# Attention and ELU-MoE on one core: a new hand-laid order, W1 loaded by other groups of columns, two V casts moved to GpSimd

## The chip, the core and the metric

The kernel runs on one core of a Trainium2 chip. A core has five engines that run side by side: TensorE (matmuls into PSUM, "PE" in the profile), VectorE ("DVE"), ScalarE ("ACT"), GpSimd ("POOL") and SyncE ("SP", which here only issues DMAs). DMA queues move data between HBM and SBUF. The metric is the device time of one execution in microseconds; before the change it is 303.02 us, the median of three runs (303.0 to 303.15).

## What is computed

The reference, cut to what matters:

```python
# q, k, v: (8 batches, 8 heads, 576 tokens, 64), fp32
q_s = exp(q - max_d q);  q_s /= sum_d q_s          # softmax over the head dimension
k_s = exp(k - max_s k);  k_s /= sum_s k_s          # softmax over the tokens
kv  = einsum('bhsd,bhse->bhde', k_s, v)            # 64 x 64 a head
att = einsum('bhsd,bhde->bhse', q_s, kv)
x   = att.transpose(0, 2, 1, 3).reshape(4608, 512)
h   = x @ w_in                                     # 512 -> 2048
g   = where(h > 0, h, exp(min(h, 0)) - 1)          # ELU
out = g @ w_out                                    # 2048 -> 512
```

## The kernel before

**Two streams of work.** The attention goes by units: a unit is one batch and half of the heads, so there are 16, numbered n, two a batch. The product with w_in and w_out goes by blocks of 512 tokens: 9 blocks, numbered j. A ring XT of three blocks holds attention's output, transposed, for the products.

**A unit** (`stage1` and after it): loads of Q, K and V (576 KB each); exp of Q and of K on ScalarE (L355, L359); a cast of V to bf16 into VB (L368 on ScalarE, L371 on another engine); on VectorE the row sums of Q, their reciprocals and the scaled Q as fp16 (L375, L379, L383: QS). QS is transposed: in units 0 to 3 by TensorE (`tp`, L406), with a copy out of PSUM to qsT; from unit 4 on by a DMA issued by SP (`turn`, L422) and widened to fp32 by ScalarE (`widen`, L434). K times V is a block of 36 small matmuls (`kv_mm`, L458); VectorE scales the result to MBLK (`m`: L467, two of L471). Then `ao_mm` (L489) multiplies MBLK by qsT, and `xt` copies the result to XT (L511 on ScalarE, L514 on VectorE).

**A block** has eight groups g of 256 columns of w_in. `hg_mm` (L545) is one group: eight matmuls of 512 columns into one of four pairs of PSUM banks. `hg` empties it: exp on ScalarE (L561), two VectorE operations (L578, L580), or, in every other group of blocks 0 and 1, a second ScalarE operation (L572) and one of VectorE (L574); the result is GT. Then `out_mm` (L590) multiplies GT by w_out, 64 matmuls a block, into four output tiles; `out_store` copies a tile out of PSUM (L607, OSBX in block 0, OSB later), and SP stores it (L617). In block 0 the output tiles are made in quarters, each of which needs one of four loads of w_out (W2, 1 MB each).

**The start.** SP loads Q, K and V of units 0 and 1. GpSimd's queue loads w_in (W1) behind them, in pieces by groups: 0-2 (in two halves of the rows, so that the first half's product can begin once unit 0 is done, since unit 0 gives one half of XT's rows and unit 1 the other), 3-4 and 5-7. Each piece is two DMAs. `hg_mm` with `half` set is half a group, four matmuls. In the first microseconds TensorE gets spin matmuls on the identity (L655) where the planner sees it idle; their number follows from the planner's times.

**The order.** Every operation has an index, given by the place where `program` adds it. The table ORDER has one line of indices for each engine, and each engine runs its operations in just that order. `Sched.order` walks through the five lines with estimated durations and latencies; from the estimated starts come the interleaving in which code is emitted, and the number of spin matmuls (`fill`). Semaphore waits follow from the tiles that operations read and write. An engine works in order: what stands behind a waiting instruction waits too. The same holds for the DMA issues in the lines of SP and GpSimd. GpSimd's line in the old table, from index 57 on, reads: Q of unit 2, W2 part 0, W2 part 1, Q of 3, V of 2, K of 2, W2 part 2, K of 3, the V cast of unit 2, W2 part 3, V of 3, V of 4, Q of 4, Q of 5, the V cast of unit 3, K of 4, V of 5, K of 5. V of units 2, 4 and 5 share one buffer, so V of unit 5 can only be loaded once V of unit 4 has been cast; K of unit 4 needs unit 2's K times V to be done, K of unit 5 that of unit 3.

Where V is cast is chosen in `first`: `vconv="gp" if n < CASTS else "act"`, with CASTS = 4; units 0 and 1 have their own setting (CAST0, CAST1). W1 is loaded by

```python
for g0, g1, half in ((0, 3, 0), (0, 3, 1), (3, 5, None), (5, 8, None)):
    self.load_w1(g0, g1, half, -30, [gate, self.ident] if half == 0 else ())
```

where `gate` is the load of K of unit 0.

Of the kernel before, what the change touches and what calls it, by code (L numbers as in the profile page):

```python
# [19 lines left out]
CASTS = 4  # L20
# [4 lines left out]
        "30 28 32 45 43 47 50 68 54 67 70 71 69 72 82 86 93 103 115 128 90 129 130 138 137 107 131 "  # L25
        "139 136 109 150 149 126 134 151 132 157 158 156 140 152 153 146 173 175 172 159 174 233 239 "
        "238 237 243 192 244 245 250 251 249 201 256 257 203 255 263 262 212 261 268 267 269 321 309 "
        "313 317 333 220 325 338 329 350 334 280 399 282 342 346 291 391 351 395 299 412 400 404 408 "
        "362 417 364 425 413 430 421 438 373 479 426 381 434 487 500 439 450 483 492 452 488 496 505 "
        "461 501 513 469 509 526 514 518 522 564 538 527 568 540 572 577 549 573 581 585 590 556 594 "  # L30
        "586 598 607 599 603 640 611 636 612 644 622 649 624 645 657 653 632 670 634 662 658 666 675 "
        "683 688 679 671 709 692 714 696 684 705 701 697 718 735 710 731 740 722 727 723 744 748 761 "
        "736 753 766 749 757 774 779 762 770 787 775 783 788 792 793 797 801 805 "),
    "act": (
        "3 22 33 23 31 24 34 29 44 35 48 55 73 76 77 79 83 84 87 94 95 104 97 116 117 119 91 92 108 "
        "98 127 120 133 135 163 166 160 181 154 147 179 205 230 231 169 176 189 180 234 188 240 241 "
        "191 246 273 252 253 202 258 211 204 264 213 265 215 270 284 214 310 314 218 217 318 221 322 "
        "355 279 326 339 330 294 281 335 290 283 343 347 292 297 293 392 296 352 300 396 366 376 401 "
        "361 375 363 405 379 409 443 378 418 454 414 365 372 374 431 422 427 382 435 480 466 449 440 "
        "464 451 484 531 542 493 489 453 460 463 506 497 462 467 502 510 470 515 519 537 523 565 551 "  # L40
        "539 528 552 569 541 548 550 578 574 555 582 616 554 595 587 557 608 626 604 591 600 641 621 "
        "613 637 623 625 631 646 650 654 633 659 663 667 676 689 635 680 672 693 685 706 698 715 702 "
        "719 732 711 741 728 724 745 737 750 754 767 758 763 780 771 776 784 789 794 798 802 806 808 "),
    "dve": (
        "4 5 0 6 7 2 25 26 27 37 38 39 40 41 42 46 36 49 51 52 53 56 74 75 78 80 81 85 88 89 96 105 "
        "106 100 101 102 122 123 124 118 110 111 112 141 142 143 155 148 182 183 184 232 177 178 206 "
        "235 207 236 208 193 242 194 195 196 197 247 198 248 254 259 274 275 260 266 276 271 272 311 "
        "285 312 286 319 320 287 356 222 223 327 224 328 225 226 331 227 332 336 337 357 358 344 345 "
        "348 349 353 354 301 397 398 302 367 402 303 304 368 305 306 403 369 410 411 444 455 445 456 "
        "415 446 416 423 424 383 384 385 386 387 428 429 388 457 436 437 441 442 485 486 532 490 533 "  # L50
        "491 498 499 543 503 504 534 471 472 511 473 512 474 516 475 544 476 517 545 524 525 529 530 "
        "570 571 575 583 584 617 576 618 619 596 597 588 589 558 559 609 610 560 601 602 642 627 643 "
        "561 562 628 563 629 614 615 647 648 655 656 660 668 669 661 681 682 673 674 694 695 686 687 "
        "707 708 699 700 720 721 712 733 713 734 725 726 746 738 739 747 751 759 752 760 764 765 772 "
        "773 777 778 785 786 "),
    "gp": (
        "1 14 15 16 17 18 19 20 21 59 57 58 63 61 60 62 64 99 66 65 125 113 144 121 114 186 145 "),
    "sp": (
        "8 9 10 11 12 13 165 162 167 187 164 185 200 210 171 161 209 168 170 190 199 216 278 315 277 "
        "324 219 288 316 341 228 229 289 295 360 298 359 323 307 340 377 308 394 371 406 370 393 419 "  # L60
        "447 407 390 389 380 433 420 448 432 459 482 458 494 465 481 495 478 477 535 468 520 546 566 "
        "567 536 508 553 507 579 547 521 592 580 620 630 639 605 593 652 638 651 606 690 678 664 677 "
        "665 703 717 691 704 729 742 716 730 743 755 769 781 756 790 791 768 782 795 799 796 804 803 "
        "800 807 "),
# [3 lines left out]
class Op:  # L68
    __slots__ = ("eng", "dur", "emit", "deps", "key", "idx", "start", "end",
                 "dma", "sem", "val", "clock", "nbytes", "follow", "side", "late", "packet", "margin",  # L70
                 "gate", "span", "behind")

    def __init__(self, eng, dur, emit, key, dma=None, nbytes=0):
        self.eng, self.dur, self.emit, self.key = eng, dur, emit, key
        self.deps = {}
        self.dma, self.nbytes = dma, nbytes
        self.start = self.end = None
        self.behind = None
        self.follow, self.side, self.packet, self.margin = None, 0, 4608, 0


class Sched:
# [3 lines left out]
    LAT = {"pe": 200, "act": 138, "dve": 116, "gp": 155}  # L86
    LAND = 350
    RESTART = 110
# [40 lines left out]
    def order(self):  # L129
# [4 lines left out]
        while any(line.values()):  # L134
            before = len(seq)
            for e in self.ENG:
                while line[e]:
# [6 lines left out]
                    wake = self.RESTART if e == "pe" and t > free[e] + 30 else 0  # L144
                    o.start, o.end = t, t + o.dur + wake
# [11 lines left out]
    def hop(self, d, o):  # L157
        if d.dma:
            return 30
        if d.eng == o.eng and (d.eng == "pe" or o.deps[d] == "war"):  # L160
            return 0
        return self.LAT[d.eng]

# [79 lines left out]
class Gen:  # L243
# [85 lines left out]
    def load_w1(self, g0, g1, half, key, after=()):  # L329
        w = self.w_in.rearrange("(h kc d) f -> h d kc f", h=2, d=D)  # L330
        sl = slice(g0 * 256, g1 * 256)
        ks = slice(0, 4) if half is None else slice(2 * half, 2 * half + 2)
        xs = (0, 1) if half is None else (half,)
        for h in range(2):
            self.S.add("gp", ISSUE["gp"], lambda e, h=h: e.dma_start(
                self.W1[h:128:2, ks, sl], w[h, :, ks, sl]), key,
                W=[f"W1_{g}{x}{h}" for x in xs for g in range(g0, g1)],
                dma=f"w1{g0}{xs[0]}{h}", nbytes=(len(xs) * (g1 - g0) << 17) * (1.25 if g0 == 3 else 1), after=after,
                follow=self.gpq)
            self.gpq = self.S.ops[-1]  # L340
# [86 lines left out]
    def widen(self, n, key):  # L427
# [3 lines left out]
        if n < CASTS:  # L431
# [5 lines left out]
    def side(self, ps, key, *parts):  # L437

        def mm(e):
            for p in parts:  # L440
# [3 lines left out]
                   X=[f"b{2 * ps}", f"b{2 * ps + 1}"], side=1)  # L444

    KV = 382

    def kv_mm(self, n, ps, at=KV):
        i = n % 2
# [11 lines left out]
        return 510 if at == self.KV else 280, [f"kR{i}", f"VB{i}", f"VB{i}x", f"VBone{i}"], mm  # L461
# [160 lines left out]
    def program(self):  # L622
# [10 lines left out]
        for g0, g1, half in ((0, 3, 0), (0, 3, 1), (3, 5, None), (5, 8, None)):  # L633
# [115 lines left out]
        for half in range(2):  # L749
            for g in range(3):  # L750
                self.hg_mm(0, g, turns[g], key, half)
                S.ops[-1].follow = kv1
        for g in range(8):
            self.hg(0, g, turns[g], key, "da"[g % 2], g > 2)
# [86 lines left out]
```

## Time and profile before

| what | value |
|---|---|
| median of 3 runs | 303.02 us |
| profiled execution | 302.01 us |
| its span, first to last instruction | 300.2 us |
| mean granted TensorE clock | 0.997 |
| first matmul of L545 | 15.42 us |
| last matmul ends | about 296.7 us |
| GpSimd (POOL) busy | 20.2 us, 31 instructions |
| bytes by the two main DMA queues | 34.09 MB and 15.47 MB |

The profile is of one execution, slower or faster than the median by what runs differ. Lines of it read: engine, source line, operation, written tile <- read tiles, shapes, count. In the timeline the first column is the start and the second the length, both in us; what stands in brackets is the idle time of the engine before the row and what ended it. The chain of waits is followed back from the last instruction, at each step to what released it; its rows are start, length, what. DMA rows end with the KB of one and the median us from issue to landing. Idle time of an engine that does not bound the kernel costs nothing. Profiled lengths of matmuls overlap; the distance from one start to the next is what one costs.

### The profile page before, as it was taken

To read this page: it belongs to the slowest core of one execution; us is meant where nothing else is said; L and a number is where in the kernel's file an instruction comes from. 1 tells how busy PE (TensorE), PEld (TensorE's weight loads), DVE (VectorE), ACT (ScalarE), POOL (GpSimd) and SP (SyncE) were. 2 spreads that over 40 slices of the span, in tenths; PEclk is the share of its full clock that TensorE was granted. 3 is DMA by queue.
4 is the path that set the end of the run, shared out by engine and by line. 5 is a ranking of instruction groups with operands and counts; after the bars stand their busy time and mean duration, and the time that the engine had idled before them with its cause. 6 is when DMAs were issued, how large, how long until landed. Compare 5 with 4: busy or idle time off the path is not lost.

```text
span 300.2 us, 4428 instructions
## 1 busy us (share of the span) xinstructions
PE 286.4 (95%) x1855; PEld 234.2 (78%) x1855; DVE 189.0 (63%) x244; ACT 182.7 (61%) x213; POOL 20.2 (7%) x31
## 2 busy tenths in 40 slices
PE   0799999999999999999999999999999999999995
PEld 0678887777888888888888878888888888888883
DVE  3858934987896596787687567675344546356500
ACT  5858759988976889668937664555441543233311
POOL 0950343000000000000000000000000000000000
PEclk9999999999999999999999999999999999999998
DMA  7999999795769697368477730324030032111133
GB/s 265 385 400 388 391 340 328 232 215 211 214 154 330 177 244 218 81 213 291 131 174 180 212 114 2 75 57 107 0 86 2 0 72 60 27 36 36 35 88 87
DMA packets 35283, 49.96 MB, mean 166 GB/s; under 512 B 16320, under 2 KB 16320, under 8 KB 35264
## 3 DMA queue, kind: packets, MB, share of 16 engines
q1 hardware_dynamic: 29680, 34.09, 41.1%
q0 software_dynamic: 5504, 15.47, 15.9%
q8 instruction: 14, 0.23, 0.3%
q10 hardware_dynamic: 80, 0.13, 0.1%
q14 instruction: 5, 0.04, 0.0%
HBM read 36.70 MB, written 9.44 MB: 154 GB/s over the span
## 4 chain that ended last, share of the span: by engine, by line
PE 88%; ACT 6%; DMA 3%; DVE 2%; issue 0%; SPq 0%
PE PS L590 41%; PE PS L545 41%; PE PS L489 3%; PE PS L458 2%; DMA out_dram<-OSB 2%; ACT QR L355 1%; DMA QR<-in_q_dram 1%; ACT ESB L561 1%; PE PS L406 1%; ACT VB L368 1%; ACT KR L359 1%; PE PS L655 1%; ACT OSB L607 1%; DVE QS L383 0%; DVE ZQ L375 0%; ACT XT L511 0%
## 5 line engine op out<-in xcount | busy, mean ns | idle before, releaser
L590 PE MATMUL PS<-W,GT 128*128 128x512 f32 x576 | 141.7, 392 | 0.0
L545 PE MATMUL PS<-XT,W 128*128 128x512 f32 x576 | 140.4, 392 | 0.7 <-ACT OSBX L607 0.6
L545 PEld LDWEIGHTS PS<-XT,W 128*128 128x128 f32 x576 | 106.8, 188 | 24.4 <-ACT OSBX L607 1.0
L590 PEld LDWEIGHTS PS<-W,GT 128*128 128x128 f32 x576 | 106.6, 188 | 22.2 <-ACT OSB L607 0.6
L561 ACT ACTIVATE ESB<-PS 128x1024 f32<-128x1024 f32 x72 | 73.6, 1027 | 64.5 <-PE PS L545 64.4
L578 DVE TENSOR_SCALAR ESB<-ESB 128x1024 f32<-128x1024 f32 x64 | 44.1, 690 | 70.6 <-ACT ESB L561 70.4
L580 DVE TENSOR_TENSOR GT<-ESB,PS 128x1024 fp32r<-128x1024 f32 x64 | 77.6, 1218 | 1.7
L607 ACT ACTIVATE OSB<-PS 128x512 f32<-128x512 f32 x32 | 18.8, 598 | 23.6 <-PE PS L590 19.0
L511 ACT ACTIVATE XT<-PS 128x512 fp32r<-128x512 f32 (+6 forms) x32 | 19.3, 607 | 15.3 <-PE PS L489 13.9
L375 DVE TENSOR_REDUCE ZQ<-QR 128x18 f32<-128x1152 f32 x16 | 21.5, 1346 | 6.0 <-ACT QR L355 6.0
L383 DVE TENSOR_TENSOR QS<-QR,RZQ 128x1152 f16<-128x1152 f32 x16 | 21.7, 1355 | 0.3
L355 ACT ACTIVATE QR<-QR 128x1152 f32<-128x1152 f32 x16 | 18.4, 1166 | 3.0 <-DMA QR<-in_q_dram 3.0
L359 ACT ACTIVATE KR<-KR 128x1152 bf16<-128x1152 f32 x16 | 18.6, 1163 | 1.2 <-DMA KR<-in_k_dram 1.2
L434 ACT ACTIVATE qsT<-QT 128x1152 fp32r<-128x1152 f16 x12 | 14.0, 1170 | 3.3 <-DMA QT<-QS 2.7
L368 ACT ACTIVATE VB<-VR 128x1152 bf16<-128x1152 f32 (+1 forms) x14 | 15.9, 1132 | 0.0
L489 PE MATMUL PS<-qsT,MBLK 128*128 128x320 f32 (+5 forms) x64 | 14.0, 305 | 0.3 <-DVE MBLK L471 0.2
L489 PEld LDWEIGHTS PS<-qsT,MBLK 128*128 128x128 f32 x64 | 11.6, 189 | 3.4 <-DVE MBLK L471 0.6
L574 DVE SCALAR_TENSOR_TENSOR GT<-PS,ESB 128x1024 fp32r<-128x1024 f32 x8 | 9.8, 1222 | 3.0 <-ACT ESB L572 2.9
L406 PE MATMUL PS<-ID,QS 128*128 128x128 f16 x36 | 3.2, 243 | 8.9 <-DVE QS L383 8.9
L471 DVE TENSOR_TENSOR MBLK<-PS,RZK 64x128 fp32r<-64x128 f32 x32 | 9.2, 287 | 0.9
L406 PEld LDWEIGHTS PS<-ID,QS 128*128 128x128 f16 x36 | 2.4, 109 | 9.3 <-DVE QS L383 8.9
L572 ACT ACTIVATE ESB<-ESB 128x1024 f32<-128x1024 f32 x8 | 8.5, 1060 | 0.2
(28 smaller groups left out, 57.9 us busy)
## 6 DMA issues: line engine op xcount, KB each, us to landing
out_dram<-OSB SPq DMA_DIRECT2D x63, 128.0 KB, 2.4
QR<-in_q_dram SPq DMA_DIRECT2D x12, 576.0 KB, 4.7
KR<-in_k_dram SPq DMA_DIRECT2D x12, 576.0 KB, 5.1
VR<-in_v_dram SPq DMA_DIRECT2D x12, 576.0 KB, 5.2
W<-in_moe_w_out_dram POOLq DMA_DIRECT2D x4, 1024.0 KB, 16.1
QR<-in_q_dram POOLq DMA_DIRECT2D x4, 576.0 KB, 11.2
VR<-in_v_dram POOLq DMA_DIRECT2D x4, 576.0 KB, 7.5
KR<-in_k_dram POOLq DMA_DIRECT2D x4, 576.0 KB, 13.1
```

The source lines that it names most:

```text
L355: S.add("act", t_act(1152, False), lambda e: e.activation(flat(q), flat(q), AF.Exp), key - 3, X=[f"qR{i}"], follow=self.table)
L359: S.add("act", t_act(1152, False), lambda e: e.activation(ek[:, :, :, :].rearrange("p h c d -> p (h c d)"), flat(k), AF.Exp), key - 2, X=[ ...
L375: S.add("dve", t_dve(1152), lambda e: e.tensor_reduce(self.ZQ[i][:, :, :].rearrange("p h c -> p (h c)"), q[:, :, :, :].rearrange("p h c d ...
L383: S.add("dve", t_dve(1152), lambda e: e.tensor_tensor(qso, q[:, :, :, :], rz, ALU.mult), key - 3, R=[f"qR{i}", f"RZQ{i}"], W=[f"QS{self.al ...
L489: last = e.matmul(P[:, y:y + n_], M[:, f, :], T[:, c0:c1, f * 64:f * 64 + 64], start=True, stop=True)
L511: S.add("act", t_act((h1 - h0) * n_, True), lambda e, dst=dst, src=src: e.activation(dst, src, AF.Copy), key, W=W, X=X)
L545: last = e.matmul(P[:, t * 512:(t + 1) * 512], self.W1[:, kc, tt * 128:(tt + 1) * 128], self.XT[:, kc, rc:rc + BLK], start=(kc == 0), stop ...
L561: S.add("act", t_act(1024, True), lambda e: e.activation(esb[:, :], P[:, :], AF.Exp), key, W=[f"E{i}"], X=banks)
L578: S.add("dve", t_dve(1024, 2), lambda e: e.tensor_scalar(esb[:, :], esb[:, :], 1.0, -1.0, ALU.min, ALU.add), key, X=[f"E{i}"])
L580: S.add("dve", t_dve(1024), lambda e: e.tensor_tensor(gt, esb[:, :], P[:, :], ALU.max), key, R=[f"E{i}"], W=gw, X=banks)
L590: last = e.matmul(dst, GT[:, jj, ts * 128:(ts + 1) * 128], self.W2[:, jj, :], start=(jj == 0), stop=(jj == 15))
L607: S.add("act", t_act(512, True), lambda e: e.activation(osb[:, :], src, AF.Copy), key, W=[f"O{i}0", f"O{i}1"], X=[f"b{bk}"])
```

## The change

W1 comes in pieces of groups 0-1 (in two halves), 2-4 and 5-7. So only groups 0 and 1 of block 0 are computed in halves, and group 2 is one whole product of eight matmuls. CASTS is 6: the V casts of units 4 and 5 go to GpSimd. `widen` asked the same constant and now asks for `n < 4`; as it is only called from unit 4 on, widening stays on ScalarE. The planner's estimates change: latencies by engine, with 160 ns more for a wait of TensorE and 35 ns for others, in place of a fixed latency and a restart charge; K times V is put at 615 or 290 ns in place of 510 or 280; a block of such matmuls may count as done 200 ns early; the surcharge on a W1 piece moves from 3-4 (1.25) to 2-4 (1.15). A planner's hint that half products follow unit 1's K times V is gone. The table ORDER is replaced by another, solved for two sets of durations together.

```diff
-CASTS = 4
+CASTS = 6
...
     "gp": (
-        "1 14 15 16 17 18 19 20 21 59 57 58 63 61 60 62 64 99 66 65 125 113 144 121 114 186 145 "),
+        "1 14 15 16 17 18 19 20 21 57 59 58 60 63 61 62 66 98 64 65 112 113 124 120 144 143 180 185 "
+        "188 "),
...
-    LAT = {"pe": 200, "act": 138, "dve": 116, "gp": 155}
+    OVER = {"pe": 163, "act": 105, "dve": 82, "gp": 110}
...
-                    wake = self.RESTART if e == "pe" and t > free[e] + 30 else 0
-                    o.start, o.end = t, t + o.dur + wake
+                    o.start, o.end = t, t + o.dur
...
-        if d.dma:
-            return 30
-        if d.eng == o.eng and (d.eng == "pe" or o.deps[d] == "war"):
+        if d.eng == o.eng and not d.dma and (d.eng == "pe" or o.deps[d] == "war"):
             return 0
-        return self.LAT[d.eng]
+        return (0 if d.dma else self.OVER[d.eng] - d.early) + (160 if o.eng == "pe" else 35)
...
-                dma=f"w1{g0}{xs[0]}{h}", nbytes=(len(xs) * (g1 - g0) << 17) * (1.25 if g0 == 3 else 1), after=after,
+                dma=f"w1{g0}{xs[0]}{h}", nbytes=(len(xs) * (g1 - g0) << 17) * (1.15 if g0 == 2 else 1), after=after,
...
-        if n < CASTS:
+        if n < 4:
             self.S.add("gp", 1500, lambda e: e.tensor_copy(dst, src), key, R=["QT"], W=W)
...
+        self.S.ops[-1].early = 200 * any(p[0] > 600 for p in parts)
...
-        return 510 if at == self.KV else 280, [f"kR{i}", f"VB{i}", f"VB{i}x", f"VBone{i}"], mm
+        return 615 if at == self.KV else 290, [f"kR{i}", f"VB{i}", f"VB{i}x", f"VBone{i}"], mm
...
-        for g0, g1, half in ((0, 3, 0), (0, 3, 1), (3, 5, None), (5, 8, None)):
+        for g0, g1, half in ((0, 2, 0), (0, 2, 1), (2, 5, None), (5, 8, None)):
...
-            for g in range(3):
+            for g in range(2):
                 self.hg_mm(0, g, turns[g], key, half)
-                S.ops[-1].follow = kv1
         for g in range(8):
-            self.hg(0, g, turns[g], key, "da"[g % 2], g > 2)
+            self.hg(0, g, turns[g], key, "da"[g % 2], g > 1)
```

The first parts of the four other lines of ORDER, old against new:

```diff
     "pe": (
-        "30 28 32 45 43 47 50 68 54 67 70 71 69 72 82 86 93 103 115 128 90 129 130 138 137 107 131 "
+        "30 28 32 45 43 47 50 67 54 68 69 70 77 81 85 92 114 102 89 128 136 127 135 129 137 106 130 "
...
     "act": (
-        "3 22 33 23 31 24 34 29 44 35 48 55 73 76 77 79 83 84 87 94 95 104 97 116 117 119 91 92 108 "
+        "3 22 33 23 24 29 31 34 35 44 48 55 71 74 75 78 82 83 86 93 94 96 103 115 90 91 118 97 116 "
...
     "dve": (
-        "4 5 0 6 7 2 25 26 27 37 38 39 40 41 42 46 36 49 51 52 53 56 74 75 78 80 81 85 88 89 96 105 "
+        "4 0 5 2 6 7 25 26 27 37 38 39 40 41 42 36 49 46 51 52 53 56 72 73 76 79 80 84 87 88 95 99 "
...
     "sp": (
-        "8 9 10 11 12 13 165 162 167 187 164 185 200 210 171 161 209 168 170 190 199 216 278 315 277 "
+        "8 9 10 11 12 13 184 186 161 164 163 170 167 189 199 198 208 166 169 160 209 215 276 277 315 "
```

To read them: 24 is the V cast of unit 0, 29 and 31 are the two copies of its transposed Q; 36 is VectorE's half of the V cast of unit 1, 46 its half of the copy of unit 1's transposed Q, 49 and 56 its halves of XT of units 0 and 1; 40 to 42 and 51 to 53 scale K times V of units 0 and 1; 32 and 50 are those K times V, 47 and 54 the products with MBLK. 67 and 68 are the first halves of groups 0 and 1 of block 0 in both tables. Above 81 the new table's index is the old one less one: at the seam of blocks 0 and 1 TensorE's line reads 173 175 172 159 174 in the old table and 172 174 158 171 173 in the new one, that is, the last quarter of the last output tile of block 0 comes ahead of the first half of group 0 of block 1. In the same place ScalarE's new line has the exp of unit 4's Q (178) ahead of the XT copies of unit 3 (153, 146), and GpSimd's new line reads from 57 on: W2 part 0, Q of unit 2, W2 part 1, K of 2, Q of 3, V of 2, W2 parts 2 and 3, the V cast of unit 2, K and V of 3, Q, K and V of 4, the V cast of unit 3, K and Q of 5, the V cast of unit 4, V of 5, the V cast of unit 5.

## The prediction

> **What bounds the kernel now.** I read the page's busy table first:
>
> ```profile
> span 300.2 us, 4428 instructions
> PE 286.4 (95%) x1855; PEld 234.2 (78%) x1855; DVE 189.0 (63%) x244; ACT 182.7 (61%) x213; POOL 20.2 (7%) x31
> ```
>
> TensorE is the bound. In the chain of waits 16 matmuls of 512 columns take 3.63 us in quiet stretches, 0.2267 each; 1152 of them are 261 us. They run from 15.42 to 296.67, 281.3 us, and the 20 us between are attention's own matmuls and short restarts. So a new order can win only where TensorE really waits, and the start-to-start times show few such places: the head before 15.42, 0.73 us at 52.96, 0.28 at 177.2, and some 0.12 each after a block of small matmuls. The head by the timeline:
>
> ```profile
> 12.65 0.61 DVE L471 TENSOR_TENSOR MBLK<-PS,RZK 64x128 fp32r<-64x128 f32 x2
> ...
> 13.29 0.69 DVE L416 CAST qsT<-PS 128x512 fp32r<-128x512 f16 x1
> ...
> 14.02 0.76 DVE L371 CAST VB<-VR 128x576 bf16<-128x576 f32 x1
> ...
> 14.69 0.68 DVE L514 CAST XT<-PS 128x512 fp32r<-128x512 f32 x1
> ...
> 15.42 1.21 PE L545 MATMUL PS<-XT,W 128*128 128x512 f32 x4
> ```
>
> VectorE is a solid chain here; the first product waits for its half of XT. Under the head the DMA queues run at about 395 GB/s, so the landings of W1 matter. The DMA view, cut at single issues, of the two loads of groups 3-4 (issued at 10.50 and 11.12), the pair of groups 5-7, and what else ran from 18 to 20 us:
>
> ```profile
> W<-in_moe_w_in_dram POOLq DMA_DIRECT2D x1, 512.0 KB, 7.3
> ```
> ```profile
> W<-in_moe_w_in_dram POOLq DMA_DIRECT2D x1, 512.0 KB, 9.5
> ```
> ```profile
> W<-in_moe_w_in_dram POOLq DMA_DIRECT2D x2, 768.0 KB, 11.5
> ```
> ```profile
> q8 instruction: 1, 0.02, 3.6%
> ```
>
> The first lands at 17.82, the second at 20.61: 2.79 us for 0.52 MB, where 395 GB/s needs 1.33. Of its sixteen semaphore increments fifteen are there by 19.17; the last comes 1.44 us later, right after a 16 KB instruction packet began at 18.41 on one DMA engine. The later loads keep that lag (5-7 ends at 24.54). Before, nothing paid for it: group 3 starts near 21.6, group 5 near 25.2.
>
> **The change part by part.** Above 81 an index of the new table is the old one less one, since one half product is gone (I name operations, not indices). What the planner's constants change is the order and the number of spin matmuls; no other instruction.
>
> *Head.* ScalarE now casts V of unit 0 before it copies the transposed Q. V landed at 2.27 + 6.84 = 9.1, so the cast (1.16) ends at 10.3 instead of 11.2, and K·V can be done by about 11.5. VectorE, free at 11.81 (10.45 + 1.36), need not idle until 12.45: M of unit 0 ends at 12.65 instead of 13.26. Then VB1 0.76, XT 0.69 (ahead of the qsT copy now), qsT 0.69, M of unit 1 0.81: 15.7 instead of 16.19. ScalarE's half of XT still comes near 14.8, so the first product starts near 14.85, and the second half of the first group at 17.35 to 17.6 instead of 17.87. The spin before K·V shrinks from 18 to an estimated 8 to 10 matmuls of 107 ns, but some now stand before the transposes, hence the spread. **-0.4 us.**
>
> *W1.* Groups 0-1 take 1.05 MB instead of 1.57 first; both halves were early anyway (14.52 and 16.48), worth nothing. But group 2 now needs the whole 2-4 load, whose end is the same 2.62 MB into the stream as that of 3-4: 19.17 without the lag, 20.61 with it. TensorE wants it at 17.47 + 8 x 0.2267 + 0.11 = 19.39. Where would the fetch fall? It came after 131 matmul records, ten of them main ones; with a similar spin it comes at the tenth main matmul again, near 17.9. The Trainium skill (Runtime: NRT & Kernel Launch, section on instruction fetch mechanics) calls the cost of crossing a 16 KB block "mostly hidden". By that rule group 2 has its data at 19.2 and waits for nothing; by the row it waits 1.27 and starts at 20.66, where the same point before was 17.87 + 1.92 = 19.79. I take the row: **+0.87 net of the head.** Groups 5-7, at 24.54, are wanted at 26.1 then: free.
>
> *W2 and loads on POOL's queue.* W2's last quarter is issued before the V cast of unit 2, not behind it (36.41 before), and lands near 38.64 + 2.7 = 41.3 instead of 42.77; K and V of unit 3 move behind and land near 42.8 and 44.3 (40.09 and 44.23 before). V of unit 3 is what its K·V waits for, so nothing moves. K of unit 2 comes 3 us earlier, V 1.5 us later (35.98; its cast ends by 37.9, wanted at 39.6).
>
> *The boundary of block 0 and 1.* The chain of waits there:
>
> ```profile
> 48.51 0.74 ACT XT L511 x2
> 49.24 2.11 ACT QR L355 x2
> 51.35 0.92 ACT ESB L561
> ...
> 52.30 1.06 ACT ESB L572
> 53.36 0.49 ACT OSBX L607
> ...
> 53.90 3.94 PE PS L545 x16
> ```
>
> TensorE waited for ScalarE to empty a bank of the last output tile. That tile is now computed before, not after, the first half of group 0, so its copy has 1.8 us of cover: **-0.85** (0.73 and a 0.12 restart). What is late next is ScalarE itself. It loses V's cast of units 4 and 5 (2 x 1.05 in the chain's pitch), but the exp of unit 4's Q (1.05) now stands ahead of unit 3's XT copies, which group 1's second half needs: about +0.4. And two exps (unit 5's Q and K) stand before the exp of group 2 of block 1, as a cast and an exp did before; followed by its two VectorE steps (0.69 + 1.22) it frees group 4's banks at 60.3 to 61.1, against the start at 60.57 now: 0 to +0.7. Together **+0.6**, bounds 0 and +1.1.
>
> *Casts on GpSimd.* The two rows there are
>
> ```profile
> 34.54 1.92 POOL L371 CAST VB<-VR 128x1152 bf16<-128x1152 f32 x1 [15.70 <-DMA VR<-in_v_dram]
> ...
> 44.28 1.15 POOL L371 CAST VB<-VR 128x1152 bf16<-128x1152 f32 x1 [4.25 <-DMA VR<-in_v_dram]
> ...
> 48.61 0.72 POOL L318 DMA_DIRECT2D VR<-in_v_dram  x1 [2.51 <-ACT VB L368]
> ```
>
> The Trainium skill (SBUF — State Buffer, section on the two separate sides) speaks against this: a GpSimd operation and a VectorE one with two SBUF inputs lock a shared port pair for a whole instruction. The slow row stands beside the Q multiplication at 34.10 (1.36), the fast one alone, so the lock explains 0.77. By the rows two casts cost 2.3 to 3.8 us of GpSimd, hidden while V is in time; by the rule, if each meets a full 1.36, some 5.0. The order is what counts: V of unit 5 is issued behind unit 4's cast, which stands behind the loads of K and Q of unit 5, and K's waits for unit 3's K·V (47). So cast 4 ends at 50 to 51, V of unit 5 is issued then, not at 48.61, lands near 55.5 (54.62 before) and is cast by 57.4, when the K·V of units 4 and 5 is wanted at 58.7. No cost by a 1.3 us margin. Widening stays on ScalarE as it was: zero. SP's queue starts with unit 4's transpose ahead of block 0's stores; their tiles are overwritten only near 70 us.
>
> *The rest.* Counting matmuls between two uses of a bank pair in both tables, the least cover is 3.47 us in both, so I expect no new steady stall; the 0.28 at 177 probably goes. -0.2, bounds -0.4 and +0.8.
>
> **Sum**, against the profiled execution's 302.01 (its span 300.2 and 1.8 around it): +0.87 - 0.85 + 0.6 - 0.2 = +0.4, 302.4. The median of the runs is 303.02, so **303.4**.
>
> **Rivals.** *The fetch misses the load* (301.9): if the instruction packet comes after about 18.6, or very early on a lane with slack, group 2 starts on time: -0.4 - 0.85 + 0.3 - 0.2 = -1.1. For it: the fetches come at irregular distances (94 to 339 PE instructions), and a shorter spin delays the count by up to ten matmuls. Against: both loads of the stream stay in flight from 11 to 19 us, a wide target. *GpSimd's chain sets the pace* (304.4): the load of V of unit 5 lands after 57, because the new K and Q loads and block 0's stores go ahead of it, or both casts meet VectorE's two-input steps; then K·V of units 4 and 5 stands at the head of TensorE's order and holds everything, about +1.0 on the forecast. It decides from 1.3 us of lateness on. For it: POOL works in order and three waits are now strung on it. Against: the load took 6.0 us to land before, and 6.5 may pass now. *A stall elsewhere* (from 304): the table is new in some 200 places of TensorE's order and I have followed the first 62 us only.
>
> **Chances.** Forecast 0.40, fetch misses 0.28, GpSimd's chain 0.25, elsewhere 0.07. About 0.2%, 0.6 us, is what a measurement of this kernel can tell from no change. The first rival gives 0.24 of faster, the forecast's lower edge (its own range is 302.7 to 304.1) 0.06: 0.30 faster; the two slow cases and the forecast's upper edge give 0.36 slower; 0.34 within. The range 301.7 to 304.7 takes in both main rivals.
>
> **What would show it.** First main product near 14.85, second half near 17.5; a wait of TensorE of about 1.3 us at the fifth group of eight or so, near 20.6, ended by a W load (none: first rival); no wait near 53 for OSBX; ScalarE's exp of unit 4's Q between OSBX and XT; a TensorE wait for GpSimd's VB near 59 means the second rival. I am wrong in kind if TensorE loses time after 62 us, or if its clock is granted late because the spin is shorter.

## The result and the profile after

The kernel after the change takes **302.0 us** in the median (301.67 to 302.45); the kernel before, on the same chip, 303.01. The ratio is 0.997, with a 95% interval of 0.9957 to 0.9983. So the change made the kernel faster by about 1 us, where 0.4 us slower, 303.4, was forecast; 302.0 lies inside the stated range of 301.7 to 304.7, but on the other side of no change. A later measurement of the two unchanged kernels gave 302.03 against 302.85, ratio 0.9978 [0.9965, 0.999].

One thing has to be seen before any line of the profile is compared. The profiled execution of the kernel after took 302.05 us, as its median. That of the kernel before took 302.01, and so lay 1.0 below its own median; of 139 other executions of that kernel on record, with a median of 302.95, two were faster. So the trace that the prediction read was a rare fast execution, and from page to page nothing was gained:

```profile
span 300.2 us, 4404 instructions
...
PE 285.5 (95%) x1846; PEld 234.1 (78%) x1846; DVE 188.8 (63%) x244; ACT 181.5 (60%) x211; POOL 22.1 (7%) x33
```

The span is the same 300.2 us. GpSimd has 22.1 us instead of 20.2, ScalarE 1.2 us less. The waits of TensorE in the kernel after, behind the first one of 9.1 us for the first scaled Q (engine and line, what it waited for, us in all, times, longest):

```profile
PE PS L543 <- DMA W<-in_moe_w_in_dram: 1.3, 1, 1.3
PE PS L543 <- DVE XT L512: 0.4, 1, 0.4
PE PS L543 <- DVE GT L578: 0.2, 1, 0.2
```

A wait for W1 is there that the kernel before did not have; the wait for OSBX is gone. (Lines after are two or three lower than those of before: L545 is now L543, L590 is L588, L607 is L605.) The timeline of TensorE in the head:

```profile
14.78 1.16 PE L543 MATMUL PS<-XT,W 128*128 128x512 f32 x4 [0.42 <-DVE XT L512]
16.05 0.74 PE L487 MATMUL PS<-qsT,MBLK 128*128 128x512 f32 x2
16.63 3.05 PE L543 MATMUL PS<-XT,W 128*128 128x512 f32 x12
20.96 0.73 PE L543 MATMUL PS<-XT,W 128*128 128x512 f32 x2 [1.28 <-DMA W<-in_moe_w_in_dram]
```

The first product starts at 14.78 instead of 15.42. Group 2 waits 1.28 us for the second load of groups 2-4, whose fifteenth increment came at 19.63 and whose last came at 20.92; an instruction packet of 16 KB had begun at 18.36. The boundary of blocks 0 and 1, on ScalarE, on GpSimd and on TensorE:

```profile
52.73 0.60 ACT L605 ACTIVATE OSBX<-PS 128x512 f32<-128x512 f32 x1
...
55.47 1.16 ACT L352 ACTIVATE QR<-QR 128x1152 f32<-128x1152 f32 x1
56.53 1.15 ACT L356 ACTIVATE KR<-KR 128x1152 bf16<-128x1152 f32 x1
57.59 1.94 ACT L559 ACTIVATE ESB<-PS 128x1024 f32<-128x1024 f32 x2
```
```profile
49.96 1.16 POOL L368 CAST VB<-VR 128x1152 bf16<-128x1152 f32 x1
...
57.10 1.15 POOL L368 CAST VB<-VR 128x1152 bf16<-128x1152 f32 x1 [4.95 <-DMA VR<-in_v_dram]
```
```profile
52.53 5.60 PE L543 MATMUL PS<-XT,W 128*128 128x512 f32 x24
...
59.42 0.78 PE L456 MATMUL PS<-VB,KR 64*64 64x65 bf16 x72
```

TensorE runs 24 matmuls through the place where it waited for OSBX. ScalarE never waits for a landing here; GpSimd waits 4.95 us for V of unit 5 and delays no one, since its cast ends at 58.25 and K·V of units 4 and 5 comes at 59.42.

**Where TensorE loses time.** From the starts in each trace one can work out a loss: the distance from a matmul's start to the next start, less 0.2267 us per 512 columns (the pitch of a quiet stretch), for matmuls of 192 columns and more. Summed by stretch of the span (in us), with the time of the profiled execution and the start of the first main product:

```
profiled kernel       us    first   15.3-30  30-50  50-57  57-70  70-170  170-182  182-end
before              302.01  15.42    0.45    1.02   0.88   0.52   2.02    0.63     0.40
before, again       304.24  15.72    0.50    1.36   0.87   1.77   2.09    0.82     0.42
after               302.05  14.78    2.18    0.97   0.05   1.08   1.65    0.04     0.49
after, again        302.49  14.93    2.16    0.96   0.06   1.08   1.94    0.04     0.49
after, old W1       300.81  15.33    0.52    0.99   0.01   1.08   1.65    0.03     0.49
```

### The profile page after: what moved, and what is told of

Read it like the earlier page. It is cut to its first block, busy times and chain, and to the rows that moved or that the text cites. A ratio compares the mean times of both kernels' runs of the same rounds, so it can differ in the third digit from the quotient of the medians.

```text
span 300.2 us, 4404 instructions
## 1 busy us (share of the span) xinstructions
PE 285.5 (95%) x1846; PEld 234.1 (78%) x1846; DVE 188.8 (63%) x244; ACT 181.5 (60%) x211; POOL 22.1 (7%) x33
## 4 chain that ended last, share of the span: by engine, by line
PE 88%; DMA 5%; DVE 4%; POOL 1%; ACT 1%; SPq 0%; issue 0%
PE PS L588 43%; PE PS L543 40%; DMA W<-in_moe_w_in_dram 3%; PE PS L487 3%; DMA KR<-in_k_dram 2%; PE PS L456 1%; DVE GT L578 1%; POOL W L332 1%; DVE ESB L576 1%; DVE QS L380 0%; DVE ZQ L372 0%; DVE GT L572 0%; DVE MBLK L469 0%; ACT ESB L559 0%; PE PS L403 0%; SPq L315 0%
## 5 line engine op out<-in xcount | busy, mean ns | idle before, releaser
L543 PE MATMUL PS<-XT,W 128*128 128x512 f32 x576 | 140.8, 391 | 1.9 <-DMA W<-in_moe_w_in_dram 1.3
L588 PE MATMUL PS<-W,GT 128*128 128x512 f32 x576 | 141.2, 391 | 0.0
L543 PEld LDWEIGHTS PS<-XT,W 128*128 128x128 f32 x576 | 106.9, 188 | 25.1 <-DMA W<-in_moe_w_in_dram 1.7
L588 PEld LDWEIGHTS PS<-W,GT 128*128 128x128 f32 x576 | 107.1, 188 | 21.9 <-DVE GT L572 0.3
L605 ACT ACTIVATE OSB<-PS 128x512 f32<-128x512 f32 x32 | 18.6, 596 | 23.8 <-PE PS L588 23.8
L365 ACT ACTIVATE VB<-VR 128x1152 bf16<-128x1152 f32 (+1 forms) x12 | 13.5, 1125 | 0.8 <-DMA VR<-in_v_dram 0.8
```

The lines of the kernel that those rows point to most:

```text
L543: last = e.matmul(P[:, t * 512:(t + 1) * 512], self.W1[:, kc, tt * 128:(tt + 1) * 128], self.XT[:, kc, rc:rc + BLK], start=(kc == 0), stop ...
L588: last = e.matmul(dst, GT[:, jj, ts * 128:(ts + 1) * 128], self.W2[:, jj, :], start=(jj == 0), stop=(jj == 15))
L605: S.add("act", t_act(512, True), lambda e: e.activation(osb[:, :], src, AF.Copy), key, W=[f"O{i}0", f"O{i}1"], X=[f"b{bk}"])
```

## The experiments

All times are medians. In the short diffs the numbers are operations in the numbering of the kernel before. V casts: 181 (unit 4), 189 (unit 5); 186 the load of V of unit 5; 185 the transpose of unit 4's Q; exps of K: 180 (unit 4), 188 (unit 5); exps of Q: 179, 205; 176 and 234 the exps of groups 0 and 2 of block 1; 169 a copy of OSBX; 159 the last output product of block 0.

**1. Both kernels again, and the W1 loads by themselves.**

> The kernel before, unchanged, once more. Its first profiled execution took 302.01 us, 1.0 below its own median of 303.01, while the changed kernel's took 302.05, its own median. Theory 1: the kernel before has a stall that comes in most executions and was missing in the profiled one; then a new profile of it, if near 303, has a span near 301.2 and one new wait of TensorE of 0.5 to 1.2 us. Theory 2: the profiled execution was typical inside the span and the difference lies around it; then the span is 300.2 again at a time of 303.

> The changed kernel, unchanged, once more. Both theories: about 302.0 and 0.997 of the kernel before. In the profile the wait of 1.3 us for W1 near 20 us is there again if it belongs to the instruction packet that delays one DMA engine; if it was a chance of that execution it is gone.

The third has the change with the old W1 loads:

```diff
-for g0, g1, half in ((0, 2, 0), (0, 2, 1), (2, 5, None), (5, 8, None)):
+for g0, g1, half in ((0, 3, 0), (0, 3, 1), (3, 5, None), (5, 8, None)):
...
-for g in range(2):
+for g in range(3):
     self.hg_mm(0, g, turns[g], key, half)
```

> The changed kernel with W1 loaded by groups 0-2, 3-4, 5-7 again and group 2 of block 0 in halves again; everything else as changed. Theory that the W1 pieces cost 1.28 us on TensorE's path: the wait near 20 us goes and the time falls by 0.9 to 1.3, to 300.7 to 301.1. Rival: what follows (VectorE's chain from 54 to 67 us, the landing of V of unit 3) takes the gain back; then the time falls by less than 0.5.

Measured: before 302.99, after 302.03, after with the old W1 loads **301.08** (300.64 to 301.52; ratio to before 0.9947 [0.9933, 0.9961]). The new W1 loads cost about 0.95 us, and without them the change is faster than both kernels.

The second profile of the unchanged kernel before was the surprise. ScalarE and TensorE there:

```profile
56.83 1.17 ACT L368 ACTIVATE VB<-VR 128x1152 bf16<-128x1152 f32 x1 [1.37 <-DMA VR<-in_v_dram]
...
59.87 1.15 ACT L359 ACTIVATE KR<-KR 128x1152 bf16<-128x1152 f32 x1
...
61.07 0.78 PE L458 MATMUL PS<-VB,KR 64*64 64x65 bf16 x72 [1.19 <-ACT KR L359]
```

V of unit 5 landed at 56.81 (54.62 in the first profile), ScalarE stood in order before its cast, the exp of unit 5's K came behind it, and TensorE waited 1.19 us at the head of its order. In the first profile this chain is the same, but V came just early enough, so that no wait showed:

```profile
54.65 1.17 ACT L368 ACTIVATE VB<-VR 128x1152 bf16<-128x1152 f32 x1
...
57.70 1.16 ACT L359 ACTIVATE KR<-KR 128x1152 bf16<-128x1152 f32 x1
```
```profile
59.13 0.78 PE L458 MATMUL PS<-VB,KR 64*64 64x65 bf16 x72
```

From it came a theory: an ordinary execution of the kernel before pays about 1 us here, and the casts on GpSimd take it away. (This second profile, 304.24, is of the slowest execution among that measurement's 12; it shows what can be lost here, not what the median loses.)

**2. The casts alone, their place alone, and the reverse.**

```diff
-"act": ... 160 181 154 ... 176 189 180 234 188 ...   "gp": ... 114 186 145
+"act": ... 160 154 ... 176 180 234 188 ...           "gp": ... 114 145 181 186 189
```

> The kernel before, with the V casts of units 4 and 5 on GpSimd (unit 5's K issued ahead of unit 4's cast, V of unit 5 behind it) and the rest of its order kept. Theory (an ordinary execution of the kernel before pays about 1 us because ScalarE stands in order behind the late V of unit 5): the wait of K.V of units 4 and 5 for the exp of K of unit 5 near 59 us is gone in the profile and the median falls by 0.7 to 1.2, to 301.8 to 302.3, with less spread. Rival (the gain of the change sits in the seam and the head, the casts are worth nothing as predicted): 302.8 to 303.1.

Measured 302.95, ratio 1.0006 [0.9994, 1.0019]: the theory failed in this form. The wait for the exp of K was gone, and another stood in its place (timeline, two rows of VectorE and one of TensorE):

```profile
61.56 1.36 DVE L384 TENSOR_TENSOR QS<-QR,RZQ 128x1152 f16<-128x1152 f32 x1 [1.53 <-DMA QT<-QS]
...
62.91 1.20 DVE L575 SCALAR_TENSOR_TENSOR GT<-PS,ESB 128x1024 fp32r<-128x1024 f32 x1
...
64.17 1.20 PE L546 MATMUL PS<-XT,W 128*128 128x512 f32 x4 [1.17 <-DVE GT L575]
```

The transpose of unit 4's Q, issued on SP behind a load and a store, landed at 61.53. VectorE stood 1.53 us before its next scaling of Q, which writes a QS tile again and waited for that landing, and the GT that TensorE needs came behind it in VectorE's order. (ScalarE waited for it too, 0.53 us before the widening, but did not hold TensorE.)

```diff
-"act": ... 176 189 180 234 188 ...
+"act": ... 176 180 188 189 234 ...
```

> The kernel before with one operation moved on ScalarE: the V cast of unit 5 stands behind the exps of K of units 4 and 5, not ahead of them; it stays on ScalarE. Theory (it is the place in ScalarE's order behind a late load that costs, not the engine): most of the gain of the casts on GpSimd comes by this too, 301.9 to 302.4; the profile shows no wait for the exp of K of unit 5 near 59, at most a short one for the cast of V. Rival (ScalarE's load of two casts, 2.1 us, is what costs): 302.8 to 303.2.

Measured 303.87, ratio 1.0034 [1.0023, 1.0046]: slower than before, both accounts missed. The exp of group 2 (234) then stands behind two exps of K and the cast, and TensorE waits 0.6 us for a GT of VectorE; that this is the whole loss is not shown.

```diff
-"act": ... 163 179 154 ... 176 205 188 234 ...       "gp": ... 144 181 186 189
+"act": ... 163 181 179 154 ... 176 189 205 188 234   "gp": ... 144 186
```

> The kernel after with the two V casts back on ScalarE, at the places they have in the kernel before (unit 4's behind the second copy out of the last output tiles, unit 5's behind the exp of group 0 of block 1). Theory: ScalarE waits for V of unit 5, which lands near 57, and the exp of K of unit 5 comes late: slower than the kernel after by 1 to 2 us, 303.0 to 304.0. Rival (the casts are worth nothing): 302.0 to 302.3.

Measured 304.44, 2.4 us slower than the kernel after, more than expected. At 50.12 TensorE lost 1.86 us, because V of unit 4 lands later in this order (near 49.3) and ScalarE waited 1.11 us for it. So this place was bad in itself; section 6 puts it better.

**3. W1 alone in the kernel before.**

> The kernel before with W1 loaded by groups 0-1, 2-4 and 5-7 and group 2 as one product behind groups 0 and 1. Theory: group 2 waits some 0.9 to 1.3 us near 20.5 for the second load of groups 2-4; median 303.8 to 304.2 against 302.9. Rival (the later start of the main products in the kernel before, 15.4 instead of 14.8, covers half of it): 303.2 to 303.5.

Measured 303.46, single executions from 302.69 to 306.02, ratio 1.0028 [1.0009, 1.0048]. Its profiled execution has no wait for W at all: the instruction packet came at 19.19, when the 2-4 load had only 0.6 us to go; it was in at 19.76, and the next load bore the lag (fifteenth increment 21.67, last 22.72). So in a single execution this load order can cost 1.3 us or nothing, and where the packet falls is one thing that decides it.

**4. The packet moved in the kernel after.**

```diff
-self.PS[0][:, 0:128], self.ID[:, :], self.ID[:, :], start=True, stop=True)
-for _ in range(count)][-1]
+self.PS[0][:, 0:256].rearrange("p (r c) -> p r c", r=2), self.ID[:, :],
+self.ID[:, :].unsqueeze(1).broadcast_to([128, 2, 128]), start=True, stop=True)
+for _ in range(count // 2)][-1]
```

> The kernel after with half as many spin matmuls in the head, each of 256 columns instead of 128: nine instructions fewer, so the first instruction packet falls some nine main matmuls later, near 20.4, when the loads of groups 2-4 are in. Theory (the packet causes the wait for W1): the wait of 1.3 to 1.4 us at the ninth main batch falls to 0 to 0.4, and the loads of groups 5-7 bear the lag without anyone waiting: 300.7 to 301.3. Rival (the load is late by itself, by the spread of its sixteen increments, the packet only adds the last 0.1 to 1.3): 301.5 to 302.0.

Measured 301.57, ratio 0.9949 [0.993, 0.9968]. In the profiled execution (300.84) the packet came at 19.05 and the wait was gone:

```profile
16.85 5.33 PE L543 MATMUL PS<-XT,W 128*128 128x512 f32 x22
```

22 matmuls run through the place. The median got back only 0.45 of the 0.95, between the two accounts; the first product also came later here, at 15.01. The packet is enough to cause the wait, but in single executions (300.82 to 302.37) the load is late without it too: in the second profile of the kernel after its increments were spread from 19.35 to 20.94 before the last came at 21.07.

**5. Steps of the boundary and the head, one at a time, from the kernel before.** The casts with the transpose first in SP's order:

```diff
-"sp": ... 165 162 167 187 164 185 ...
+"sp": ... 165 162 167 185 187 164 ...
```

> The kernel before with the V casts of units 4 and 5 on GpSimd and, in SP's order, the transpose of unit 4's Q ahead of the load of unit 6's Q and of one store. Theory (the chain at the boundary of the blocks hangs by two landings that ScalarE awaits in order, V of unit 5 and the transpose of unit 4; with the casts alone the second took the place of the first): both waits gone, the transpose lands near 58, no loss of TensorE over 0.4 us between 58 and 66; 301.8 to 302.3. Rival (the waits there are not what the medians differ by): 302.7 to 303.0.

Measured 302.5, ratio 0.9981 [0.9962, 1.0]: half of what was expected, and at the edge of no change. The transpose landed in 3.08 us (5.3 to 7.1 behind the load and the store), and 57-70 lost 0.55.

```diff
-"pe": ... 173 175 172 159 174 ...   "act": ... 230 231 169 176 ...
+"pe": ... 173 175 159 172 174 ...   "act": ... 230 169 231 176 ...
```

> The kernel before with the last output product of block 0 ahead of the first half of group 0 of block 1, and its copy out on ScalarE one step earlier. Theory: the wait for OSBX near 53 goes (0.72 and a restart of 0.12), but what comes next, the K.V of units 4 and 5, hangs by landings that do not come earlier for it, so that part of it is lost again: 302.3 to 302.6. Rival one (it counts in full): 302.0. Rival two (all of it is lost again): 302.8 to 303.0.

Measured 302.79, ratio 0.9991 [0.9971, 1.0011], not told from no change. The loss in 50-57 fell from 0.88 to 0.16, as predicted, but 57-70 lost 1.39, of which 0.91 stands before K·V, which waited for ScalarE's exp of K.

The order of the head up to the first products, as in the kernel after:

> The kernel before with the order of the kernel after on TensorE, ScalarE and VectorE up to the start of the main products. The first main product starts near 14.9 to 15.1, where the profiles of the kernel before and its variants have 15.4 to 15.75. Theory: the gain of 0.5 to 0.7 counts in part, 302.3 to 302.6. Rival (all later waits hang by landings): 302.8 to 303.0.

Measured 303.31, ratio 1.0007 [0.9983, 1.0031]. The first product started at 14.47 and not sooner because it waited 0.58 us for W1 there; at 61.63 TensorE lost 1.37 by the same chain through VectorE as with the casts alone, behind a transpose that took 7.09 us to land.

All three boundary edits together (casts, transpose, seam):

> The kernel before with three edits at the boundary of blocks 0 and 1 together: the V casts of units 4 and 5 on GpSimd, the transpose of unit 4's Q first in SP's order there, and the last output product of block 0 ahead of group 0 of block 1. Theory (alone each wait removed gives its place to the next one; together the 0.85 of the seam counts in full beside the 0.3 to 0.5 of the casts with the transpose): 301.5 to 301.9; no loss of TensorE over 0.4 us from 50 to 66. Rival (they add up as measured alone, -0.5 and -0.2): 302.2 to 302.4.

Measured 302.92, ratio 1.0007 [0.9994, 1.002]. Both accounts missed. Rows of ScalarE and of TensorE in its profile show what is late next:

```profile
57.03 1.03 ACT L562 ACTIVATE ESB<-PS 128x1024 f32<-128x1024 f32 x1 [1.19 <-DVE GT L581]
57.96 1.15 ACT L360 ACTIVATE KR<-KR 128x1152 bf16<-128x1152 f32 x1
```
```profile
59.16 0.78 PE L459 MATMUL PS<-VB,KR 64*64 64x65 bf16 x72 [0.46 <-ACT KR L360]
```

ScalarE stood idle for 1.19 us before the exp of group 2, with the exp of unit 5's K ready behind it. The kernel after has that exp of K first (56.53 in its rows above). With this exchange, and the same kind of exchange near 176 (exp of unit 15's K ahead of that of unit 14's Q):

```diff
-"act": ... 176 180 234 188 ... 616 554 ...
+"act": ... 176 180 188 234 ... 554 616 ...
```

> The kernel before with the three edits at the boundary, and two more on ScalarE: the exp of unit 5's K ahead of the exp of group 2 of block 1, and near 176 us the exp of unit 15's K ahead of the exp of unit 14's Q. Theory (with these no K.V waits for an exp that stands behind another in order): the loss of 0.52 near 58 and of 0.46 near 177 go, 301.7 to 302.1. Rival (the medians differ by something that these waits do not show): 302.7 to 303.0.

Measured **302.09**, ratio 0.9971 [0.9957, 0.9985]: the upper end of the theory. It keeps the head and the W1 loads of before, and has the gain of the whole change. In the two profiles the place of the gain is not the first exchange: K·V's wait of 0.46 is gone, but 57-70 loses 1.11 and 1.10, since other short waits come instead. It is the second: 170-182 loses 0.97 without and 0.48 with it, though ScalarE waits as long for the landing of a store at 172 (1.29 and 1.28 us). TensorE's row there, without and with the exchange:

```profile
178.14 0.50 PE L490 MATMUL PS<-qsT,MBLK 128*128 128x256 f32 x2 [0.40 <-ACT KR L360]
```
```profile
177.71 0.40 PE L490 MATMUL PS<-qsT,MBLK 128*128 128x256 f32 x2
```

So 0.5 of the 0.83 between the medians is seen in that stretch. The profile without the exchanges (302.49) lay 0.43 below its own median, and where the rest went is not seen.

Two kernels were to price the later order by itself: the kernel before, and the last but one, up to the third output group of block 1, with the order of the kernel after from there on.

> The kernel before up to about the third output group of block 1, and from there on the order of the kernel after on TensorE, ScalarE, VectorE and SP. Theory: the loss near 177 to 179, which was 0.12 to 0.83 in nine profiles of the kernel before and its variants (0.48 in the mean) and is absent from all of the kernel after, goes: 302.4 to 302.6. Rival (it costs nothing in the median): 302.8 to 303.0.

> Both: the three edits at the boundary and the later order of the kernel after; only the head and the W1 loads are those of the kernel before. Theory: 301.1 to 301.5, which leaves 0 to 0.4 for the head against the 301.08 that the kernel after has with the old W1 loads. Rival (the head is worth 0.8 or more): 301.8 to 302.2.

Measured 311.13 and 311.67. Where the two orders are joined, loads on SP's queue come too late (ScalarE waited 2.77 us for a V and 5.70 us for a K), so they price the joint and say nothing of the later order as such.

**6. One step undone where the others are in place.** Each starts from the change with the old W1 loads (301.08). The seam undone:

> The kernel after with the old W1 loads (301.08 before), and the seam undone: the last output product of block 0 behind the first half of group 0 again, its copy out one step later on ScalarE. Theory (where ScalarE waits for no landing, the seam counts in full): the wait for OSBX of 0.5 to 0.7 and its restart come back, +0.6 to +0.9, 301.7 to 302.0. Rival (worth the 0.2 that it had in the kernel before): 301.2 to 301.4.

The casts on ScalarE, each where I thought it best:

```diff
-"act": ... 154 147 180 ... 205 188 234 ...           "gp": ... 181 186 189
+"act": ... 154 147 181 180 ... 205 188 189 234 ...   "gp": ... 186
```

> The kernel after with the old W1 loads, and the V casts of units 4 and 5 on ScalarE, each at the best place I see: unit 4's behind the XT copies of unit 3, unit 5's behind the exp of unit 5's K. Theory (ScalarE is the chain from 50 to 60 us, and the 2.1 us of the two casts lie on it): +0.7 to +2.0, 301.8 to 303.1, TensorE waiting near 60 for the exp chain of group 2. Rival (only the order of the exps and landings counted, the casts fit in): 301.0 to 301.4.

The head of the kernel before:

> The kernel after with the old W1 loads, and the head of the kernel before on TensorE, ScalarE and VectorE. Theory: the head is worth the 0.4 predicted: 301.4 to 301.6. Rival: nothing, 301.0 to 301.2, or 0.8 and more, from 301.9.

Measured: seam undone 301.0 (the rival was nearer), casts undone **302.57** (as the theory had it), head undone 301.23 (less than expected, and with six executions each, 301.01 to 301.31 against 300.64 to 301.52, not told from nothing). With the casts back on ScalarE, its rows and the matmul that waits:

```profile
56.02 1.19 ACT L355 ACTIVATE KR<-KR 128x1152 bf16<-128x1152 f32 x1
57.07 1.19 ACT L364 ACTIVATE VB<-VR 128x1152 bf16<-128x1152 f32 x1
58.13 1.96 ACT L558 ACTIVATE ESB<-PS 128x1024 f32<-128x1024 f32 x2
```
```profile
61.22 3.93 PE L542 MATMUL PS<-XT,W 128*128 128x512 f32 x16 [0.81 <-DVE GT L577]
```

V of unit 5 had landed at 55.97, so no landing was late: ScalarE is simply full from 47 to 62 (busy 14.91 of the 15 us; 14.52 without the casts), and its exps, with VectorE's steps behind them, come about a cast too late. With the seam undone but the casts on GpSimd, ScalarE copies OSBX out nearly in time (its row, and TensorE's):

```profile
52.47 0.58 ACT L605 ACTIVATE OSBX<-PS 128x512 f32<-128x512 f32 x1
```
```profile
52.07 4.95 PE L543 MATMUL PS<-XT,W 128*128 128x512 f32 x20
```

TensorE goes through the place where the kernel before lost 0.71; 50-57 loses 0.28.

## Why the prediction was wrong

Two steps failed. What the casts take off ScalarE was entered as no gain; put back on ScalarE, they cost 1.5 us. And a sum worked out against an execution of 302.01 was added to a median 1.0 higher. Most of the other steps came true in the trace, some by luck. Point by point, against the kernel before's profiled execution:

- *Head, -0.4.* The first product came at 14.78 (14.85 said), and the second half of the first group at 17.58 (17.35 to 17.6 said, 17.87 before). Of the 0.64 won at the first product 0.35 was lost again, most of it (0.28) in a wait for VectorE's MBLK of unit 1. In the median the head is worth 0.15 (301.23 against 301.08), not clear of noise.
- *W1, +0.87 net of the head.* Right by the row: 1.28 us waited near 21 where 1.27 was worked out. In the median the loads cost 0.95. The Trainium skill (Runtime: NRT & Kernel Launch, instruction fetch mechanics) has such a crossing "mostly hidden"; here it was not, since a load that TensorE needed came late behind the packet, and moving the packet by 0.7 us took the wait out of the profiled execution.
- *W2 and the loads: nothing.* No run tried this alone; no wait for them shows in the trace.
- *Boundary, -0.85 and +0.6.* In the profile -0.83 (50-57) and +0.56 (57-70). The second size is luck: neither step that was named for it cost anything to speak of (50-57 loses 0.05, so the XT copies were in time, and near 60.5 TensorE has one restart of 0.11), while 0.34 was lost at 66.1, in a wait for VectorE's GT that was not foreseen. And the cause of the first was put in the wrong place. The wait for OSBX was "for ScalarE to empty a bank", and the tile's earlier place was to remove it. With the casts off ScalarE this wait nearly goes without it: undoing the seam costs nothing (301.0 against 301.08). In the kernel before the seam alone gave 0.2, within noise.
- *"No cost by a 1.3 us margin", and no gain, for the casts on GpSimd.* The margin came out (the cast ended 1.17 us before K·V), though V of unit 5 landed at 57.04, 1.5 us later than said, and TensorE came 0.7 us later too. The Trainium skill's shared port pair (SBUF — State Buffer, two separate sides) cost nothing in view: each cast took 1.15 or 1.16 us, and neither ran beside a VectorE operation with two inputs in SBUF. **What failed is the zero:** the prediction priced what the casts cost GpSimd. That ScalarE loses them, 2 x 1.05 us, it did write, under the boundary, but it entered no gain for that, though ScalarE's rows filled the chain of waits from 48.5 to 53.4 that it had quoted. Put back on ScalarE in the new order, at the places tried, they cost **1.5 us** (302.57 against 301.08).
- *"The rest. -0.2."* The loss after 70 us fell by 0.87 from profile to profile (70-170 by 0.37, 170-182 by 0.59, after 182 +0.09). The prediction counted one wait of 0.28 at 177. But K·V there stands behind ScalarE's exp of K, which comes behind a wait for a store's landing (0.99 us of ScalarE's idle time at 172 in the first profile, 1.55 in another) and behind the exp of Q; nine profiles with the order of before lost 0.48 to 1.21 in 170-182, those with the whole order of after 0.02 to 0.04.
- *"The median of the runs is 303.02, so 303.4."* **This step failed most, by 1.0.** The sum's +0.4 was added to the median as if what made ordinary executions slower than the profiled one would stay. From profile to profile the time did stay (302.01 and 302.05); the median fell by 1.0. The two profiles of the same kernel, 302.01 and 304.24, differ by 1.25 in 57-70, 0.34 in 30-50, 0.3 in the head and 0.19 in 170-182: places most of which the change rewrites. In the kernel after 57-70 loses 1.08 in both profiles, and its first profiled execution lies at its median. That an execution at the median of before pays just in these places is likely, but not shown: none such was profiled.

So of the 1.4 us between 303.4 and 302.0, 1.0 is this last step, and 0.4 is in the sum itself: there "The rest" measured -0.87 where -0.2 was put, and the head with W1 +1.1 (0.64 won, 1.73 lost from 15.3 to 30) where +0.87 was. Of the rivals, the fetch that misses gave 301.9, near the result for a wrong reason: the wait for W1 was there. Its sum also put the boundary at +0.3 where the forecast had +0.6, without saying why. GpSimd's chain did not set the pace.

Undone one at a time: W1 +0.95, casts -1.5, head -0.15, seam 0, together -0.7 of the -0.96 between the medians 302.99 and 302.03. The first two are clear of noise. That the parts may be added is not shown: alone in the kernel before the casts gave nothing. The remaining 0.26 fits the later order; the two kernels that were to price it broke at their joint, but the exchange near 176 shows that an order of exps there is worth up to 0.5 in a profile. Open is also why the three boundary edits together gave nothing in the median while their profile lost less in 50-57.

## What to carry to other kernels

Before adding a forecast to a median, compare the profiled execution's own time with it: where it lies below by more than the effect in question, list the in-order steps that wait for a landing and had only just no wait, because an ordinary execution may pay there and the change may remove it. Price an operation taken off a full engine by undoing it in the order where everything else fits, not by adding it alone to the old one: alone, the casts were worth 0, and in the whole order 1.5 us. A gain from a reordering and a gain from a lighter engine can be the same wait, and are then not to be added.

## What the hardware showed that was not expected

- The transpose of unit 4's Q by DMA landed in 5.27 to 7.09 us in the seven profiles where SP issues it behind a 0.59 MB load and a store, and in 3.02 to 4.56 us in the eleven where it goes ahead of them: 3.08 to 3.37 in the order of before with this one change, 4.39 to 4.56 with the order of after, but 3.02 where the casts were put back in section 2. What sets the difference among these is open.
- In the kernel joined from two orders TensorE stood still for about 4 us, and its granted clock was then 0.60 for the next stretch (window, us, busy time and matmuls, granted clock, DMA share, GB/s):

```profile
90.00:96.00 6.00, 6.00 (x28) 1.00 0.56 122
...
100.50:104.60 4.10, 3.96 (x12) 0.60 0.47 144
```

A matmul of 512 columns took 0.427 us there instead of 0.227, from 101.5 until 104.5; in the stretch from 104.6 to 108 the granted clock was 0.98. The waits of 1.2 to 1.4 us elsewhere were followed by one longer start (0.335), and the granted clock stayed at 1.00 over the stretch.
